# Causal block attention and a gated convolution on one core: q and k loaded nine tokens a row, the last 64 tokens with the rest, and a new written-out order

## The chip, the cores and the metric

The kernel runs on 1 core of one Trainium2 chip. The metric is the device time of one execution in microseconds (us), the median of several runs. The core has five engines that work side by side: PE (TensorE), DVE (VectorE), ACT (ScalarE), POOL (GpSimd) and SP (SyncE, which here only issues DMAs). Sixteen DMA engines move data between HBM, the on-chip SBUF and back. Matrix products land in PSUM, which has eight banks of 2 KB a partition.

## The reference

There are 8 batches, 8 heads, 576 tokens and 64 values a head, in float32. Attention is causal by blocks of 64 tokens:

```python
scores = scale * np.matmul(q, k.transpose(0, 1, 3, 2))     # scale 1/8
mask = block_i >= block_j                                  # blocks of 64 tokens
attn = softmax(np.where(mask, scores, -1e9))
x = (attn @ v)          # then [B, S, H * D] = [8, 576, 512]
gate_pre += conv_w[k] * xp[:, k:k + S, :]                  # causal, five taps, per channel
out = (1 / (1 + np.exp(-gate_pre)) * (x @ w_val)) @ w_out
```

## The kernel before, in words

Each step is one small function (an op), and the text PLAN lists all of them: `S/5.1/P/4+5` is op S with arguments 5 and 1 on engine P (PE) with PSUM banks 4 and 5. Engines: P is PE, V DVE, A ACT, G POOL, S SP. Each engine works through its own words in the order of the list and waits for what they need; so the order of PLAN is the order on every engine and on SP's queue, but engines run ahead of each other freely.

The attention works by pairs of heads, `p` = 0 to 31, four to a batch. For one pair the steps are these.

- `lq`, `lk` (L258) load the first 512 tokens of two heads into `qks` (five buffers), four tokens a row: rows of 1024 B. `lt` (L281) loads the last 64 tokens of all eight heads of a batch, two tokens a row (512 B), in two transfers each for q and k. `lv`, `lvt` (L274, L288) load v.
- `cq` casts q and k of a pair to fp16 (`qk16`), mostly on POOL; `ct` does so for the tails, `cv` and `cvt` for v. All copies and casts go through one helper, so they have the line of that helper: L244 on ACT, L246 on DVE and POOL.
- `T` turns q and k of a pair by 16 transposes on PE (L141) into half of two PSUM banks, and `Te` evacuates 1024 elements a partition into `qkT` (four buffers) on DVE or ACT, putting the tokens back in order. `TT`, `TTe` do so once a batch for the tails, into `ktails` (`kt`). The first pair has its own steps `cq0`, `T0`, `T0e`.
- `S` (three parts, t = 0, 1, 2) makes the scores transposed, keys on partitions. Both heads of a pair use a half of PE's rows. Part 2 holds keys 256 to 383 and the 64 tail queries against all four key blocks. `SL` makes the scores of the tail keys for a batch.
- `E` (L458, ACT) exponentiates 1024 elements a partition into `pt`; `EL` (L474) does so for SL. `mka` and `mkb` (L481, L483, L487, POOL) then set to zero what the mask hides.
- `A` multiplies with v, 20 matmuls; a column of ones in v gives the sums. `N` (L508, L509, DVE) divides. `X` transposes back and `Xe` writes to `xt`, channels on partitions. `AT`, `NT`, `XT`, `XTe` do the same for the tail queries of a batch.

The second half works on runs of 464 columns of `xt`, `n` = 0 to 9: `C` is the convolution by 80 matmuls of 32 rows and 32 columns with diagonal weights, `CS` (L617, ACT) its tanh, `V` the product with `w_val` (four parts of four matmuls), `Ve` (L635, DVE) the gate. `O` multiplies 128 tokens with `w_out`, `Oe` evacuates, `Od` (L660, SP) stores. `C/n` needs the columns of its run, so the first convolution waits for the first batch's attention.

PSUM is shared out by hand: a pair of banks has four quarters, and `place` puts a step into free quarters (`PAIRS`: two of them, `SINGLES`: one, the three of `A`).

Of the kernel before, what the change touches and what calls it, by code (L numbers as in the profile page):

```python
# [12 lines left out]
lk/1/S ppool//G pdve//V lcv//S ccv//G CW//P/1 lq/1/A cq/1/V T/1/P/4+5 lq/0/S lk/0/S lt/0.1/S  # L13
lt/0.0/S ct/0/G lk/4/S lq/3/S CWe//V lk/3/S cq/3/G cq0/0/V T0/0/P/0+1 lq/2/S lk/2/S lq/4/S cq0/1/V
T0/1/P/2+3 Te/1/A pact//A S/1.1/P/4+5 lv/1.0/S lv/0.0/S lv/0.1/S S/1.0/P/6+7 lt/1.0/S lq/5/S
lv/2.1/S T0e/0/V lk/5/S T0e/1/A S/0.0/P/2+3 lv/1.1/S lv/2.0/S lvt/0/S lv/3.1/S lt/1.1/S TT/0/P/0+1
lk/6/S TTe/0/V lv/3.0/S lq/6/S cq/4/G E/1.1/A E/0.0/A lwv/1/S lwv/0/S SL/0/P/0+1 EL/0/A S/0.2/P/2+3
E/1.0/A S/1.2/P/4+5 E/1.2/A S/0.1/P/0+1 T/3/P/6+7 cq/2/V T/2/P/4+5 mka/1/G cv/0/G Te/3/A S/3.1/P/6+7
E/0.1/A T/4/P/0+1 Te/2/V S/2.2/P/4+5 lwo/1/S lwo/0/S E/0.2/A mka/0/G mkb/0/G lk/7/S S/2.1/P/2+3
lq/7/S lt/2.0/S Te/4/V S/4.0/P/0+1 E/3.1/A E/2.2/A E/2.1/A S/2.0/P/6+7 E/2.0/A A/0/P/4+5 S/3.2/P/6+7  # L20
cq/5/V T/5/P/2+3 lt/2.1/S lk/8/S lv/4.1/S lq/10/S E/4.0/A N/0/V cv/2/V X/0/P/4+5 mkb/1/G cv/1/G
A/1/P/0+1 lq/8/S Xe/0/V E/3.2/A S/4.1/P/4+5 N/1/V S/3.0/P/6+7 mkb/3/G mkb/2/G mka/2/G Te/5/A
S/5.0/P/2+3 lk/10/S E/4.1/A ct/1/G cv/3/G lv/4.0/S A/2/P/0+1 N/2/V lq/9/S lk/9/S lv/6.0/S E/3.0/A
mka/3/G S/5.1/P/4+5 E/5.1/A TT/1/P/6+7 TTe/1/V lv/5.1/S cvt/0/G cq/6/G A/3/P/0+1 N/3/V cwv/1/G
cwo/0/G E/5.0/A ct/2/G lv/7.1/S S/4.2/P/6+7 SL/1/P/4+5 lv/6.1/S EL/1/A mka/4/G cq/7/G E/4.2/A
mkb/4/G cq/8/G lq/13/S lv/5.0/S lv/7.0/S lvt/1/S lk/12/S lq/12/S lk/11/S lq/11/S AT/0/P/2 X/1/P/4+5
X/3/P/0+1 Xe/3/A T/6/P/6+7 Te/6/A X/2/P/0+1 Xe/2/A NT/0/V XT/0/P/3 S/6.0/P/6+7 E/6.0/A Xe/1/V
C/0/P/0+1+4+5 CS/0.1/A CS/0.0/A XTe/0/V cwv/0/V V/0.3/P/7 cwo/1/V Ve/0.3/V V/0.0/P/6 Ve/0.0/V
S/6.1/P/4+5 E/6.1/A W//P/0+1+2+3 We/0/A We/1/V S/5.2/P/6+7 TT/2/P/4+5 TTe/2/V V/0.2/P/2 SL/2/P/0+1
S/6.2/P/4+5 E/5.2/A T/7/P/6+7 Ve/0.2/V Te/7/V EL/2/A E/6.2/A V/0.1/P/0 S/7.0/P/4+5 E/7.0/A mka/5/G  # L30
T/8/P/6+7 S/7.1/P/2+3 E/7.1/A Ve/0.1/V cv/4/G A/4/P/0+1 Te/8/V S/8.2/P/6+7 N/4/V E/8.2/A O/0.2/P/4
Oe/0.2/A mkb/5/G S/8.1/P/0+1 E/8.1/A X/4/P/2+3 mka/6/G cq/10/G Xe/4/V cq/9/G T/9/P/6+7 T/10/P/6+7
Te/9/V S/8.0/P/4+5 E/8.0/A O/0.0/P/2 Oe/0.0/V S/7.2/P/0+1 E/7.2/A S/9.2/P/4+5 E/9.2/A cv/6/G mkb/8/G
Te/10/V mkb/6/G A/6/P/2+3 cv/5/G A/5/P/0+1 N/6/V mka/7/G S/9.0/P/6+7 S/9.1/P/4+5 E/9.0/A mkb/7/G
cv/7/G A/7/P/2+3 lk/13/S E/9.1/A lt/3.0/S N/5/V X/5/P/2+3 S/10.1/P/6+7 E/10.1/A lq/14/S lt/3.1/S
cvt/1/G AT/1/P/0 S/10.0/P/4+5 E/10.0/A O/0.1/P/1 Oe/0.1/A lk/14/S N/7/V Xe/5/V NT/1/V XT/1/P/0
X/6/P/6+7 Xe/6/A XTe/1/V X/7/P/2+3 cq/12/G T/12/P/4+5 cq/11/G T/11/P/4+5 lv/9.1/S S/10.2/P/0+1
E/10.2/A cq/13/G mka/9/G Xe/7/V C/1/P/2+3+6+7 lv/8.1/S CS/1.0/A ct/3/G cq/14/G mka/8/G Te/11/V
Te/12/V lv/8.0/S lq/15/S cv/8/G mkb/9/G V/1.0/P/1 Ve/1.0/V V/1.1/P/0 Ve/1.1/V CS/1.1/A lk/15/S
lv/9.0/S lt/4.1/S S/11.1/P/2+3 lvt/2/S lv/11.1/S lt/4.0/S E/11.1/A lv/11.0/S lk/17/S T/13/P/4+5  # L40
TT/3/P/4+5 lq/17/S lv/10.0/S lv/10.1/S lq/18/S lk/18/S Te/13/V S/11.0/P/6+7 E/11.0/A V/1.3/P/1
Ve/1.3/V T/14/P/2+3 Te/14/V mkb/10/G cv/9/G lv/12.0/S mka/11/G S/11.2/P/6+7 V/1.2/P/0 TTe/3/A
E/11.2/A S/13.1/P/4+5 mkb/11/G lv/12.1/S Ve/1.2/V S/14.1/P/2+3 S/13.2/P/6+7 cq/15/G A/8/P/0+1
E/13.1/A O/0.4/P/4 ct/4/G E/13.2/A S/13.0/P/6+7 N/8/V E/14.1/A lq/16/S lk/16/S Oe/0.4/V A/9/P/0+1
S/12.0/P/2+3 X/8/P/4+5 E/13.0/A T/15/P/4+5 N/9/V S/12.1/P/6+7 S/12.2/P/0+1 E/12.0/A E/12.1/A
lv/13.1/S Te/15/V Xe/8/V X/9/P/2+3 E/12.2/A cv/11/G A/11/P/2+3 N/11/V O/0.5/P/7 lt/6.1/S Oe/0.5/A
Xe/9/V S/14.0/P/5+6 mka/10/G cvt/2/G lv/13.0/S cq/17/G TT/4/P/0+1 T/17/P/0+1 X/11/P/0+1 Te/17/V
# [12 lines left out]
V/2.2/P/2 Ve/2.0/V Xe/15/V S/19.2/P/0+1 E/19.0/A Ve/2.2/V E/19.2/A Od/0.3/S lv/17.1/S lq/24/S  # L60
cq/20/G T/20/P/6+7 mka/16/G lv/16.0/S lvt/4/S lv/19.0/S ct/5/G mkb/17/G lv/17.0/S Od/0.4/S
TT/5/P/6+7 lv/19.1/S C/3/P/2+3+4+5 CS/3.0/A Te/20/V V/3.1/P/0 V/3.0/P/1 CS/3.1/A SL/4/P/2+3 TTe/5/V
SL/5/P/2+3 EL/4/A lk/23/S cq/22/G cq/21/G lk/24/S lk/25/S EL/5/A lv/20.1/S C/4/P/4+5+6+7 CS/4.0/A
Ve/3.0/V Ve/3.1/V V/3.2/P/1 Ve/3.2/V V/3.3/P/2 S/20.2/P/4+5 lq/25/S lq/27/S CS/4.1/A lk/26/S
Od/0.2/S T/21/P/0+1 TT/6/P/0+1 lt/7.0/S Od/0.1/S cv/18/G mka/19/G mkb/16/G T/22/P/6+7 E/20.2/A
cv/16/G O/1.0/P/3 Te/22/A lk/27/S lv/21.0/S mkb/19/G S/20.1/P/4+5 E/20.1/A Ve/3.3/V O/1.1/P/2
lq/26/S lv/21.1/S mkb/18/G Te/21/V S/21.1/P/6+7 A/16/P/4+5 Oe/1.0/V TTe/6/V Oe/1.1/V S/21.0/P/2+3
N/16/V cv/17/G E/21.1/A cv/19/G A/19/P/0+1 N/19/V S/21.2/P/6+7 E/21.0/A E/21.2/A S/20.0/P/4+5
A/18/P/2+3 V/4.0/P/1 cvt/4/G cq/24/G cq/23/G N/18/V E/20.0/A mka/21/G cq/25/G Ve/4.0/V S/22.0/P/6+7
E/22.0/A X/19/P/2+3 T/24/P/2+3 Xe/19/V Te/24/V lv/20.0/S Od/0.6/S lv/22.0/S lv/22.1/S T/23/P/4+5  # L70
cq/27/G lv/23.0/S A/17/P/0+1 N/17/V lvt/6/S cv/21/G mkb/21/G V/4.1/P/6 Ve/4.1/V lt/7.1/S lk/29/S
# [12 lines left out]
O/1.5/P/6 EL/7/A A/23/P/4+5 N/23/V S/24.1/P/0+1 E/24.1/A Xe/20/V V/5.2/P/7 mkb/27/G Ve/5.2/V
# [28 lines left out]
def kernel(  # L113
# [123 lines left out]
    def rot(tiles, i):  # L237
        return tiles[i % len(tiles)]
# [503 lines left out]
```

## Time and profile before

| | us |
|---|---|
| runs, median of 3 (lowest to highest) | 183.24 (182.59 to 184.49) |
| span of the profiled execution, first to last instruction | 180.0 |
| PE busy (share of the span) | 159.7 (89%) |
| ACT busy | 137.3 (76%) |
| DVE busy | 122.6 (68%) |
| POOL busy | 82.6 (46%) |
| DMA queue of SP, share of 16 engines | 76.0% |
| granted TensorE clock | 1.000 |

How to read it: the profile shows one execution. It gives that execution's span; a time of its own beside the span is not given, and the median of the runs lies 3.24 us above it. PE busy counts a matmul from its issue to its modelled end, so a busy PE can still be waiting between matmuls. Groups of instructions are named by line, engine and out<-in. "PEld" is the loading of weights into PE, which lies beside the matmuls.

### The profile page before, as it was taken

To read this page: it belongs to the slowest core of one execution; us is meant where nothing else is said; L and a number is where in the kernel's file an instruction comes from. 1 tells how busy PE (TensorE), PEld (TensorE's weight loads), DVE (VectorE), ACT (ScalarE), POOL (GpSimd) and SP (SyncE) were. 2 spreads that over 40 slices of the span, in tenths; PEclk is the share of its full clock that TensorE was granted. 3 is DMA by queue.
4 is the path that set the end of the run, shared out by engine and by line. 5 is a ranking of instruction groups with operands and counts; after the bars stand their busy time and mean duration, and the time that the engine had idled before them with its cause. 6 is when DMAs were issued, how large, how long until landed. Compare 5 with 4: busy or idle time off the path is not lost.

```text
span 180.0 us, 8228 instructions
## 1 busy us (share of the span) xinstructions
PE 159.7 (89%) x3513; PEld 98.5 (55%) x3513; DVE 122.6 (68%) x249; ACT 137.3 (76%) x162; POOL 82.6 (46%) x198
## 2 busy tenths in 40 slices
PE   0567987779989998899899999999999999999991
PEld 0343765345754665656555755566775557455450
DVE  6635665687869786669748896587984876935640
ACT  2499999889979997989798989988996753333432
POOL 6326372677674677547467437462930622000000
PEclk9999999999999999999999999999999999999999
DMA  5899899997978799969999997998796006063366
GB/s 171 255 302 228 195 326 358 267 271 171 292 223 233 175 281 243 236 200 269 296 214 273 329 275 193 293 284 224 229 319 167 0 4 230 6 232 127 117 235 232
DMA packets 66494, 40.39 MB, mean 224 GB/s; under 512 B 40213, under 2 KB 60949, under 8 KB 66458
## 3 DMA queue, kind: packets, MB, share of 16 engines
q1 hardware_dynamic: 65898, 39.35, 76.0%
q8 instruction: 27, 0.44, 1.1%
q10 hardware_dynamic: 560, 0.52, 0.9%
q14 instruction: 9, 0.07, 0.1%
HBM read 30.42 MB, written 9.44 MB: 221 GB/s over the span
## 4 chain that ended last, share of the span: by engine, by line
PE 59%; DMA 14%; SPq 9%; ACT 6%; issue 4%; DVE 3%; POOL 2%; POOLq 0%; DVEq 0%
PE PS L137 54%; PE PS L141 5%; DMA qks<-in_q_dram 5%; ACT pt L458 4%; SPq L258 4%; DMA qks<-in_k_dram 3%; DMA vs<-in_v_dram 3%; SPq L281 3%; SPq L274 2%; DMA conv_nat<-in_moe_conv_w_dram 2%; DMA vts<-in_v_dram 2%; ACT qkT L244 1%; DVE x L509 1%; DVE qkT L246 1%; POOL qk L246 1%
## 5 line engine op out<-in xcount | busy, mean ns | idle before, releaser
L458 ACT ACTIVATE pt<-PS 128x1024 f16<-128x1024 f32 x96 | 93.1, 1041 | 10.6 <-PE PS L137 9.0
L246 POOL CAST qk<-qks 128x1024 f16<-128x1024 f32 x28 | 29.0, 1041 | 18.8 <-DMA qks<-in_k_dram 9.1
L137 PE MATMUL PS<-xt,w_val 128*128 128x464 f16 x160 | 36.5, 360 | 0.5 <-DVE w_out L600 0.3
L137 PE MATMUL PS<-qkT 64*128 64x256 f16 (+3 forms) x256 | 34.0, 319 | 3.0 <-DVE qkT L246 1.2
L137 PE MATMUL PS<-w_out,gv 128*128 128x512 f16 (+1 forms) x148 | 35.6, 374 | 0.0
L635 DVE SCALAR_TENSOR_TENSOR gv<-th,PS 128x112 f16<-128x112 f32 (+4 forms) x64 | 26.1, 449 | 10.2 <-ACT th L617 5.1
L137 PEld LDWEIGHTS <-pt 128*128 128x128 f16 (+1 forms) x960 | 28.0, 103 | 8.0 <-issue 4.0
L137 PE MATMUL PS<-v,pt 128*128 128x65 f16 (+1 forms) x896 | 31.4, 196 | 0.8 <-POOL v L246 0.3
L246 DVE COPY qkT<-PS 128x1024 f16<-128x1024 f16 (+1 forms) x24 | 28.7, 1199 | 4.7 <-PE PS L141 3.0
L137 PEld LDWEIGHTS <-qkT 64*128 64x128 f16 x512 | 17.5, 98 | 16.6 <-issue 9.4
L617 ACT ACTIVATE th<-PS 128x928 f32<-128x928 f32 x20 | 17.8, 947 | 9.9 <-PE PS L137 9.5
L246 POOL CAST v<-vs 128x512 f16<-128x512 f32 x31 | 19.2, 622 | 12.0 <-DMA vs<-in_v_dram 8.7
L509 DVE TENSOR_TENSOR x<-PS,rc 128x512 f16<-128x512 f32 x32 | 22.1, 692 | 1.1
L137 PEld LDWEIGHTS <-w_val 128*128 128x128 f16 x160 | 13.9, 98 | 14.1 <-issue 2.6
L137 PEld LDWEIGHTS <-gv 128*128 128x128 f16 x148 | 13.0, 98 | 13.3 <-issue 1.5
L246 DVE COPY osb<-PS 128x512 f32<-128x512 f32 x18 | 12.4, 690 | 7.6 <-PE PS L137 5.2
L141 PE MATMUL PS<-ident,qk 64*128 64x64 f16 x512 | 13.8, 199 | 3.9 <-POOL qk L246 1.3
L246 DVE COPY xt<-PS 128x512 f16<-128x512 f16 (+1 forms) x34 | 13.1, 399 | 5.4 <-PE PS L141 3.2
L481 POOL MEMSET pt<- 64x256 f16 x32 | 9.8, 306 | 14.0 <-ACT pt L458 13.0
L244 ACT COPY osb<-PS 128x512 f32<-128x512 f32 x17 | 10.0, 586 | 7.0 <-PE PS L137 4.5
L141 PEld LDWEIGHTS <-qk 64*128 64x128 f16 x512 | 11.1, 100 | 7.2 <-POOL qk L246 2.8
L508 DVE RECIPROCAL rc<-PS 128x8 f32<-128x8 f32 x32 | 6.6, 205 | 12.2 <-PE PS L137 9.6
(62 smaller groups left out, 134.3 us busy)
## 6 DMA issues: line engine op xcount, KB each, us to landing
out_dram<-osb SPq DMA_DIRECT2D x35, 256.0 KB, 3.3
qks<-in_k_dram SPq DMA_DIRECT2D x32, 256.0 KB, 4.7
vs<-in_v_dram SPq DMA_DIRECT2D x64, 128.0 KB, 4.3
qks<-in_q_dram SPq DMA_DIRECT2D x31, 256.0 KB, 4.6
tls<-in_k_dram SPq DMA_DIRECT2D x16, 64.0 KB, 4.1
tls<-in_q_dram SPq DMA_DIRECT2D x16, 64.0 KB, 3.6
vts<-in_v_dram SPq DMA_DIRECT2D x8, 128.0 KB, 4.0
gv<-in_moe_w_val_dram SPq DMA_DIRECT2D x2, 512.0 KB, 6.9
```

The source lines that it names most:

```text
L137: made.append(nc.tensor.matmul(out=out, lhsT=lhsT, rhs=rhs, start=start, stop=stop, skip_group_check=True))
L141: made.append(nc.tensor.transpose(out=out, in_=in_, identity=identity))
L244: i = nc.scalar.copy(out=out, in_=in_)
L246: i = (nc.vector if eng == "V" else nc.gpsimd).tensor_copy(out=out, in_=in_)
L258: DMA[eng].dma_start(out=rot(qks, p)[0:128, i], in_=(q, k)[i][b, 2 * g:2 * g + 2, 0:512, 0:64].rearrange("h (p n) d -> p h (n d)", n=4))
L281: DMA[eng].dma_start(out=tls[b % 2][0:128, i, r], in_=(q, k)[i][b, 0:8, 512:576, 0:64].rearrange("(g r) (p n) d -> r p g (n d)", r=2, n=2)[r])
L458: made.append(nc.scalar.activation(out=rot(pts, p)[0:128, 0:2, 512 * t:512 * t + 512], in_=both(take("S", p, t)), func=AF.Exp, bias=0.0, s ...
L481: nc.gpsimd.memset(pt[64:128, 0:2, 0:1024].rearrange("p h (t s) -> p h t s", t=2)[:, :, :, 0:64], 0.0)
L508: made.append(nc.vector.reciprocal(out=rc[0:128], in_=r[:, :, :, 64:65]))
L509: made.append(nc.vector.tensor_tensor(out=rot(x16, p)[0:128].rearrange("p i h d -> p h i d"), in0=r[:, :, :, 0:64], in1=rc[0:128].to_broad ...
L617: made.append(nc.scalar.activation(out=rot(ths, n)[0:128, 2 * i:2 * i + 2], in_=both(take("C", n, i))[:, :, 0:RUN], func=AF.Tanh, bias=0.0 ...
L635: made.append(nc.vector.scalar_tensor_tensor(out=gv[0:128, x, a - 4 * i:e - 4 * i], in0=rot(ths, n)[0:128, x, a - o:e - o], scalar=1.0, in ...
```

## The change

q and k are handled by units of two pairs, `u` = 0 to 15, two to a batch, with all 576 tokens. One transfer loads nine tokens a row (2304 B) of one head of each of the two pairs; the rows of the two alternate over the 128 partitions. A cast `cd` takes q or k of a unit (1152 elements a partition, `cds` half of it), `Tt` turns it by 18 transposes into three quarters of two banks, `Te` evacuates 1152 elements, `Tex` the half for one pair. The tail's own path (`lt`, `ct`, `TT`, `TTe`, `byhead`, `tls`, `tl16`, `ktails`) is gone, as are `T0`, `T0e`, `cq0` and `w0`, a matmul on zeros. The last 64 queries are read straight from `qkT`, so S's third part has 8 matmuls in place of 10, on as many columns; the places of the parts in `pt` and the two memsets follow from that. The casts and evacuations have lines L247 (ACT) and L249 (DVE, POOL) after the change.

```diff
-    qks = consts(5, [128, 2, 2, 256], fp32, "qks")
-    tls = consts(2, [128, 2, 2, 128], fp32, "tls")
-    qk16 = consts(4, [128, 4, 4, 64], fp16, "qk16")
-    qkT = consts(4, [128, 2, 512], fp16, "qkT")
+    qks = [consts(3, [128, 2, 576], fp32, f"{n}s") for n in "qk"]
+    qk16 = [consts(2, [128, 9, 2, 64], fp16, f"{n}16") for n in "qk"]
+    qkT = consts(3, [128, 2, 2, 640], fp16, "qkT")
...
-    def load_qk(i, p, eng):
-        b, g = divmod(p, 4)
+    def load_qk(i, u, h, eng):
+        b, w = divmod(u, 2)
         DMA[eng].dma_start(
-            out=rot(qks, p)[0:128, i],
-            in_=(q, k)[i][b, 2 * g:2 * g + 2, 0:512, 0:64].rearrange(
-                "h (p n) d -> p h (n d)", n=4))
+            out=rot(qks[i], u)[0:128, h],
+            in_=(q, k)[i][b, 4 * w + h:4 * w + h + 3:2, 0:576, 0:64].rearrange(
+                "x (p n) d -> p x (n d)", n=9))
...
+    def cd(u, i, eng, bank=None):
+        copy(eng, rot(qk16[i], u)[0:128].rearrange("p n h d -> p h n d"),
+             rot(qks[i], u)[0:128].rearrange("p h (n d) -> p h n d", n=9))
...
+    def Tt(u, i, eng, bank):
+        o = place(bank, TRIPLES, "Tt", u, i)
+        for n in range(9):
+            halves(both16(bank), o + 64 * n, rot(qk16[i], u)[0:128, n])
...
+    def Te(u, i, eng, bank=None):
+        bank, o = placed("Tt", u, i)
+        copy(eng, rot(qkT, u)[0:128, i, 0:2, 0:576].rearrange("p x (r s n) -> p r x s n", r=2, n=9),
+             tokens(both16(bank)[:, :, o:o + 576]))
...
     def S(p, t, eng, bank):
...
-            work = [(0, 2, 256, 512)] + [(256 + 64 * j, j, None, None) for j in range(4)]
+        work = ([(0, 0, 0, 512)], [(0, 3, 384, 512), (128, 1, 128, 512)],
+                [(0, 2, 256, 576), (320, 0, 512, 576), (384, 1, 512, 576), (448, 3, 512, 576)])[t]
...
     def mka(p, eng, bank=None):
-            pt[64:128, 0:2, 0:1024].rearrange("p h (t s) -> p h t s", t=2)[:, :, :, 0:64], 0.0)
-        nc.gpsimd.memset(pt[64:128, 0:2, 896:960], 0.0)
+            rot(pts, p)[64:128, 0:2, 0:1024].rearrange("p h (t s) -> p h t s", t=2)[:, :, :, 0:64], 0.0)
...
     def mkb(p, eng, bank=None):
-        nc.gpsimd.memset(rot(pts, p)[64:128, 0:2, 1024:1088], 0.0)
+        nc.gpsimd.memset(
+            rot(pts, p)[64:128, 0:2, 640:1408].rearrange(
+                "p h (t s) -> p h t s", t=2)[:, :, :, 0:64], 0.0)
```

The whole PLAN is written anew. The preparations that stood in two words (`ppool`, `pdve`) are cut into smaller ones (`pv`, `px`, `pt`, `pd1`, `pz`) and placed later. The first transfers go on two queues, ACT's and SP's:

```diff
-lk/1/S ppool//G pdve//V lcv//S ccv//G CW//P/1 lq/1/A cq/1/V T/1/P/4+5 lq/0/S lk/0/S lt/0.1/S
+pdve//V lq/0.1/A lq/0.0/S lk/0.0/A lk/0.1/S pact//A lv/2.1/S lq/1.1/A lv/3.1/S lq/1.0/A lk/1.0/S
+cds/0.0.1/A lcv//S cds/0.0.0/A lk/1.1/S Tt/0.0/P/0+1 cds/0.1.0/G Tex/0.0.0/A Tex/0.0.1/V lq/2.0/S
```

By count of words: POOL has 24 casts `cd` and 2 `cds` in place of 28 `cq` and 8 `ct`, and 20 `cv` in place of 31; DVE has 12 `cv` in place of 1 and 6 `cd`; ACT has 8 `Xe` in place of 3, 2 `cds` and 2 `Tex`. E, EL, CS, N, Ve, Oe, A, X, C, V and O are as many as before, on the same engines.

More of the change, by code (lines that the diff above doesn't have):

```diff
@@ L18 @@
[L18 to L23, printed above, removed]
@@ L192, in placed, with half @@
         return take(*key), 256 * zs[0]
+    def half(*key):
+        if key in halved:
+            return placed(*key)
+        halved.add(key)
+        taken.append(where[key])
+        return where[key], 256 * spots[key][1][0]
+    halved = set()
     ident = const([128, 128], fp32, "ident")
@@ L312, in pdve, with pd1 @@
         nc.vector.tensor_copy(out=ident16[0:128], in_=ident[0:128])
-        for i in range(2):
-            nc.vector.memset(ktails[i][0:128, 0:4, 1:2, 64:128], 0.0)
+    @op
+    def pd1(eng, bank=None):
         for i in range(4):
@@ L317, in pdve, with pz, pv, px @@
             nc.vector.tensor_copy(out=idfold[hs, 0, 0:32], in_=ident16[hs, 32 * i:32 * i + 32])
[L318 to L324 removed]
+    @op
+    def pz(eng, bank=None):
+        for t in qkT:
+            nc.vector.memset(t[0:128, 1, 0:2, 576:640], 0.0)
+    @op
+    def pv(eng, bank=None):
         for t in v16s:
             nc.gpsimd.memset(t[0:128, 0:4, 0:2, 64:65], 1.0)
+    @op
+    def px(eng, bank=None):
+        for i in range(4):
+            nc.gpsimd.memset(xt[0:128, 0:4, slot(i):slot(i) + 4], 0.0)
+        nc.gpsimd.memset(xt[0:128, 0:4, RING:RING + 4], 0.0)
+    @op
+    def pt(eng, bank=None):
         for i in range(2):
@@ L329, in ppool @@
             nc.gpsimd.memset(v16t[i][64:128, 0:8, 64:65], 0.0)
-        for i in range(4):
-            nc.gpsimd.memset(xt[0:128, 0:4, slot(i):slot(i) + 4], 0.0)
-        nc.gpsimd.memset(xt[0:128, 0:4, RING:RING + 4], 0.0)
         for t in vts:
@@ L383, in halves @@
             turn(out=r[:, h, o:o + 64], in_=x[hs], identity=ident16[hs, hs])
-    def transposes(t, i, r, o=0):
-        for c in range(4):
-            halves(r, o + 256 * i + 64 * c, t[0:128, c, 2 * i:2 * i + 2, 0:64])
-    def in_order(r, i):
-        return r[:, :, 256 * i:256 * i + 256].rearrange("p r (n s) -> p r s n", n=4)
-    @op
-    def T0(i, eng, bank):
-        where["T0", i] = bank
-        transposes(qk16[0], i, both16(bank))
-    @op
-    def T0e(i, eng, bank=None):
-        copy(eng, qkT[0][0:128, i].rearrange("p (r s n) -> p r s n", r=2, n=4),
-             in_order(both16(take("T0", i)), i))
@@ L675 @@
     nc.vector.memset(tiny[0:128], 0.0)
-    nc.vector.memset(wz[0:128], 0.0)
     make_identity(nc, ident)
```

286 lines of the change are left out of this document (117 added, 169 removed).

## The prediction

> **What bounds the kernel now.** I read the page's busy shares and slices first, then the stretches of time, the groups, the waits, the chain, and last the timeline for where ten landmarks fall.
>
> ```profile
> PE 159.7 (89%) x3513; PEld 98.5 (55%) x3513; DVE 122.6 (68%) x249; ACT 137.3 (76%) x162; POOL 82.6 (46%) x198
> ...
> PE   0567987779989998899899999999999999999991
> ...
> DMA  5899899997978799969999997998796006063366
> ...
> q1 hardware_dynamic: 65898, 39.35, 76.0%
> ```
>
> PE is nearly full from mid-span on; before that its digits show holes. The loads keep the DMA engines at seven to nine tenths until about 138 us. The stretches show who is full while PE is not (columns: length, PE, PEld, DVE, ACT and POOL busy, clock, DMA share, GB/s):
>
> ```profile
> 15.00:20.00 5.00, 3.94 (x56) 2.46 (x57) 2.72 (x5) 5.00 (x7) 2.29 (x8) 1.00 0.88 214
> 20.00:25.00 5.00, 4.36 (x99) 3.25 (x96) 3.27 (x8) 5.00 (x6) 2.36 (x8) 1.00 0.86 252
> ...
> 100.00:110.00 10.00, 10.00 (x227) 6.13 (x226) 8.94 (x17) 8.79 (x10) 4.98 (x10) 1.00 0.93 263
> ...
> 140.00:150.00 10.00, 10.00 (x211) 5.93 (x210) 6.79 (x17) 6.21 (x8) 5.00 (x15) 1.00 0.03 10
> ```
>
> Early on ACT is busy without a gap: it exponentiates. Later PE is. The groups give the durations that I use (busy us, mean ns | idle before):
>
> ```profile
> L458 ACT ACTIVATE pt<-PS 128x1024 f16<-128x1024 f32 x96 | 93.1, 1041 | 10.6 <-PE PS L137 9.0 <-POOL qk L246 0.8 <-POOL v L246 0.3
> L246 POOL CAST qk<-qks 128x1024 f16<-128x1024 f32 x28 | 29.0, 1041 | 18.8 <-DMA qks<-in_k_dram 9.1 <-DMA qks<-in_q_dram 6.2 <-issue 2.1
> L246 DVE COPY qkT<-PS 128x1024 f16<-128x1024 f16 x23 | 28.0, 1221 | 4.6 <-PE PS L141 2.8 <-ACT pt L474 1.5
> L246 DVE COPY qkT<-PS 128x512 f16<-128x512 f16 x1 | 0.7, 691 | 0.2 <-PE PS L141 0.2
> ```
>
> The casts wait for q and k to land (9.1 + 6.2 us). How long PE itself waits for the evacuations of the transposed q and k is in the view of the tile qkT, under what ended its engine's idle time:
>
> ```profile
>   DVE qkT L246: 3.6, 8
>   ACT qkT L244: 3.1, 7
> ```
>
> The chain runs over SP's issues and landings from 24 to 68 us and is pure PE from 88 us to the end:
>
> ```profile
> 46.52 0.54 SPq L281
> 47.07 0.04 issue
> 47.11 0.60 SPq L281
> ...
> 154.54 21.78 PE PS L137 x256
> ```
>
> The landmarks are the ten convolution blocks C/0 to C/9, found in the timeline by their 80 small matmuls:
>
> ```profile
> 29.72 1.27 PE L137 MATMUL PS<-xt,DG 32*32 32x464 f16 x80
> ```
>
> They start at 29.7, 52.0, 75.1, 87.5, 91.4, 112.6, 135.5, 148.0, 159.5 and 164.8 us. From the plan I count the work listed ahead of each, with the rows' durations: PE by start-to-start times of undisturbed steps (S 0.222, A 0.614, V 0.784, O 0.864, C 1.203, sixteen transposes 0.233 us), ACT by busy time over count (E 93.1/96 = 0.970). For C/4 that is 82.3 us of ACT and 58.6 us of PE, 91.4 us after the start. So up to C/4 time runs at 91.4/82.3 = 1.11 of the ACT work ordered ahead, while PE has lost a third: until there the kernel goes at ACT's pace, with the DMA engines close by (81 us of packet time done by then, 0.89 of the clock). After C/4 PE has 136.3 − 58.6 = 77.7 us left and takes 176.4 − 91.4 = 85.0, which is 7.3 over.
>
> **The change, part by part.** *Transfers.* Before: 64 of 256 descriptors of 1024 B, and 32 of 128 of 512 B for the last 64 tokens. After: 64 of 128 descriptors of 2304 B; the bytes are the same. The trace's packet records average 18.6, 29.6, 52.9 and 90.1 ns for 256, 512, 1024 and 2048 B. A packet of 2304 B is not in the trace. The slope from 1024 to 2048 B gives 90.1 + 256 × 0.0363 = 99.4 ns; at the bytes-per-ns of the 1024 B row it would be 119 ns, at the best single rate (2048 B, median 84 ns) 94.5. I take 99.5, as 2048 is the nearest size. Over 16 engines: before (16,384 × 52.9 + 4,096 × 29.6)/16 = 61.7 us, after 8,192 × 99.5/16 = 50.9 us; 10.8 us less of some 137, bounds 0.8 and 13.3 less.
> [...]
>
> *SP.* 32 tail issues go (L281, median 0.60 us): 19 us of queue time, in a stretch where the chain runs over just these.
>
> *POOL.* Casts 28 × 1.041 + 8 × 0.615 = 34.1 become 24 of 1152 elements at 1.041 + 128 × 0.00082 = 1.146, and 2 halves: 28.9. Eleven v casts go to DVE (−6.8 us); per pair one memset of 0.199 goes and mkb's grows to 0.306 (−2.9 us in all). POOL is at 46%; this only brings casts forward.
>
> *DVE and ACT.* An evacuation of 1152 elements costs 1.221 + 128 × (1.221 − 0.691)/512 = 1.354 us on DVE and 1.14 on ACT, in place of 1.221 and 0.72 (a tail). 32 × 1152 is the old 32 × 1024 + 8 × 512 to the element, so only fixed costs go. With the moved casts and copies DVE goes from 126.0 to 131.6 us by my count, ACT from 141.7 to 144.6 (two casts, two half evacuations, five more Xe). Neither is hidden by itself; what counts is where it stands.
>
> *PE.* 32 × 18 transposes are 31 × 16 + 2 × 8 + 8 × 8 = 576 as before. S's third part has 320 + 3 × 64 = 512 columns in 8 matmuls where it had 256 + 4 × 64 in 10; steps of equal columns took equal times (0.22 to 0.24 us for 2, 4 and 10 matmuls), so I take 0, with up to 64 × 13 ns = 0.8 us gained if instructions counted. PE's work stays at 136.1 us against 136.3.
>
> *The start.* The first four transfers now go on ACT's and SP's queues, both q heads first. The first q transfer landed 3.7 us after its issue at 0.74; with 0.58 MB for both I take 4.5. In the changed kernel's instruction list ACT's fourth load waits on the completion count that its first one raises, and the casts are queued behind it: issue 0.5 us, two casts 0.64 each, to 6.3. 18 transposes (16 cold ones took 0.61) to 6.95; the halves of the evacuation go one after the other, ACT then DVE, as DVE's waits for ACT's (0.64 + 0.76), with idfold's copies queued behind; the k transposes need the same two banks and follow at 8.4; the first E starts at about 10.1 us, 8.7 before. But six E then run back to back, where before an EL, a Te and gaps lay between: by 17 us both have about seven.
>
> *The new order.* This is the largest term. Counted as above, what stands ahead of C/4 is 73.8 us of ACT, not 82.3, and 55.2 us of PE, not 58.6: fewer exponentials run ahead of the PE work that the convolutions open. The last load that a cast listed ahead of C/4 needs stands after 64.2 us of DMA time, against 75.6.
>
> *The sum.* C/4 at 73.8 × 1.11 = 82.0, plus 1.0 for the later start: 83.0 us. The loads allow it: when C/4 started before, 81.2 us of packet time were done, 5.6 more than needed; with that lead (64.2 + 5.6)/0.89 = 78.4. PE then has 136.1 − 55.2 = 80.9 us left, with the same loss (7.3 × 80.9/77.7 = 7.6): 171.5. What follows the last matmul stays (180.0 − 176.4 = 3.6): a span of 175.1, or 4.9 less. The profiled execution is known by its span of 180.0 alone; the median of the runs, 183.24, lies 3.2 above it, and I keep that: 178.3 us.
>
> **The rivals.** *More gain.* If the freed queues also remove half of the 7.6 us that PE loses late, it is 174.5. For it: POOL's casts wait 15.3 us for q and k. Against: late in the span PE's idle time is already small.
>
> *The long rows do not move faster* (119 ns a packet, or the rows are cut into smaller packets, so that the transfer doesn't do what it says). 44 transfers are needed ahead of C/4, each 128 × 19.5/16 = 0.156 us dearer: 6.9 us. With the same lead (71.1 + 5.6)/0.89 = 86.2, and C/4 comes 3.2 later: 181.5 us. [...]
>
> *The coarse unit: slower.* Two pairs now become ready together, after four transfers, two casts and two evacuations of 1.354 us, and none of their six S can start before both. Each transposition holds three quarters of two banks where T held half. PE waits 3.6 + 3.1 us for qkT now. If each of the 13 units after the first three exposed half of its two evacuations, 1.354 us, PE would wait 17.6, or 10.9 more, and the gain turns into 183.24 − 4.9 + 10.9 = 189.2 us. It wins from (4.9 + 6.7)/13 = 0.89 us a unit. For it: DVE is the fuller engine after the change and works in order. Against: qkT holds six pairs, not four, so a unit can be prepared a unit ahead.
>
> **How the numbers follow.** Forecast 0.50, more gain 0.12, no faster rows 0.12, coarse unit 0.26. The range, 173.5 to 188.0, takes in the second and third and most of the way to the coarse unit; the forecast's own is 175 to 181.4. Faster by over 1% 0.62, within 1% (about what a measurement of this kernel can tell from none) 0.12, slower 0.26.
>
> **What would show it.** Right: 8,192 packets of 2304 B near 99 ns; C/4 near 83 us; POOL's wait for q and k below 15.3 us; first E near 10. Wrong: PE's waits for qkT above 11 us, C/4 later than 88, or idle PE after 100 us above what it is now.

## The result, and the profile after

The changed kernel takes 191.73 us (median of 4 runs, 189.31 to 193.34), the kernel before beside it 183.5: a ratio of 1.037, 95% interval 1.027 to 1.046. Forecast were 178.3 us. The profiled execution has a span of 187.5 us at a granted clock of 0.997, against 180.0. Medians below are over all runs of a kernel; the ratios compare undisturbed runs alone (of the changed kernel 189.31 and 191.25 us), with the kernel before on the same chip.

The page's busy shares, slices and queues:

```profile
PE 160.9 (86%) x3448; PEld 98.7 (53%) x3448; DVE 128.6 (69%) x254; ACT 140.6 (75%) x164; POOL 72.7 (39%) x143
...
PE   0276898998899999898699969998998899989992
...
DMA  4999998999996798599970499779975419101076
...
q1 hardware_dynamic: 53082, 38.69, 72.4%
...
q8 instruction: 27, 0.44, 1.0%
```

PE's digits are no better than before up to the middle, and where the kernel before had nines from 90 us on there is now a 6 at 89 us and another at 108 (slices 20 and 24 of 4.7 us). The stretches (columns as before):

```profile
15.00:20.00 5.00, 3.69 (x64) 2.36 (x60) 4.25 (x5) 4.11 (x6) 3.45 (x12) 1.00 1.14 319
20.00:25.00 5.00, 4.65 (x81) 3.52 (x75) 3.85 (x7) 4.08 (x5) 3.42 (x11) 1.00 1.08 316
...
90.00:100.00 10.00, 8.34 (x132) 4.00 (x115) 5.04 (x10) 7.35 (x9) 3.34 (x5) 1.00 0.75 186
...
110.00:120.00 10.00, 8.16 (x135) 4.25 (x119) 3.90 (x9) 6.44 (x7) 2.32 (x4) 1.00 0.92 275
140.00:150.00 10.00, 9.02 (x230) 6.30 (x223) 7.86 (x16) 9.12 (x11) 4.24 (x10) 1.00 0.56 173
```

ACT, which had 5.00 of 5 us in the two early stretches, now has 4.1: it no longer sets the pace there. PE, which had 10.00 of 10 in every such stretch from 90 us on, loses 1.7 and 1.8 us in two of them. The groups of the exponentials, the casts and the evacuations:

```profile
L414 ACT ACTIVATE pt<-PS 128x1024 f16<-128x1024 f32 x96 | 93.2, 1026 | 11.1 <-PE PS L136 9.9 <-DVE rc L466 0.5
...
L249 DVE COPY qkT<-PS 128x1152 f16<-128x1152 f16 (+1 forms) x24 | 31.3, 1304 | 12.1 <-ACT qkT L247 7.4 <-PE PS L140 4.6
...
L249 POOL CAST k<-ks 128x1152 f16<-128x1152 f32 (+1 forms) x15 | 17.2, 1148 | 9.2 <-DMA ks<-in_k_dram 9.0
```

The chain of waits has two pieces, in the stretches above, in which PE waits for nothing that the profile shows, and is PE alone from 170 us on:

```profile
90.35 1.66 issue
...
110.39 1.84 issue
...
170.53 13.37 PE PS L136 x68
```

C/0 to C/9 start at 31.1, 48.9, 68.7, 89.2 (C/3), 88.2 (C/4), 109.3, 134.2, 152.6, 168.1 and 169.2 us. At 88 us both kernels have done the same PE work; the changed kernel lost its time after that.

To see where, I took PE's time apart: each step's start-to-start time, less its undisturbed time (lowest tenth of like steps: S 0.22 us, A 0.60, V 0.783, O 0.863, C 0.99) and less what a change between steps of 64, 128 and 32 rows costs (0.10 us; 0.21 behind C). What is left is waiting. It is a packet end if it falls where PE's next packet of instructions is due (below) and the profile names nothing that PE waited for there; otherwise it is a wait for another engine. The column of e15 is of an execution of 186.94 us, 1.4 above its median. In us:

| | before | changed | e9, 160 in front | e10, 256 in front | e15, other order |
|---|---|---|---|---|---|
| undisturbed work of PE | 133.1 | 132.5 | | | 132.5 |
| changes of rows | 14.1 | 14.0 | 14.0 | 14.0 | 16.0 |
| up to 20 us: start and all waits | 14.3 | 15.7 | | | |
| waits, 20 to 80 us | 11.2 | 10.6 | 10.6 | 11.1 | 7.7 |
| packet ends after 20 us | 0.7 | 4.3 | 0.0 | 4.8 | 3.0 |
| waits after 80 us | 2.0 | 6.1 | 7.5 | 7.0 | 6.3 |

So the 7.5 us are 3.6 of packet ends, 4.1 of waits after 80 us less 0.6 between 20 and 80, and 1.4 in the first 20 us; PE has 0.6 less to do, and a last step that is 0.5 shorter.

### The profile page after: what moved, and what is told of

Same layout as the page of the kernel before. It is cut to its first block, busy times and chain, and to the rows that moved or that the text cites. A ratio compares the mean times of both kernels' runs of the same rounds, so it can differ in the third digit from the quotient of the medians.

```text
span 187.5 us, 8012 instructions
## 1 busy us (share of the span) xinstructions
PE 160.9 (86%) x3448; PEld 98.7 (53%) x3448; DVE 128.6 (69%) x254; ACT 140.6 (75%) x164; POOL 72.7 (39%) x143
## 4 chain that ended last, share of the span: by engine, by line
PE 66%; ACT 13%; DVE 11%; issue 4%; DMA 3%; POOL 1%; ACTq 0%; DVEq 0%; POOLq 0%
PE PS L136 60%; ACT pt L414 7%; PE PS L140 6%; DVE qkT L249 4%; ACT qkT L247 4%; DVE x L467 2%; DMA qs<-in_q_dram 2%; DVE xt L249 2%; DMA vs<-in_v_dram 1%; ACT xt L247 1%; DVE rc L466 1%; DVE gv L593 1%; ACT q L247 1%; DVE w_out L558 1%; DVE v L249 0%
## 5 line engine op out<-in xcount | busy, mean ns | idle before, releaser
L414 ACT ACTIVATE pt<-PS 128x1024 f16<-128x1024 f32 x96 | 93.2, 1026 | 11.1 <-PE PS L136 9.9
L136 PE MATMUL PS<-qkT 64*128 64x64 f16 (+4 forms) x512 | 38.5, 264 | 3.6 <-DVE qkT L249 1.0
L249 DVE COPY qkT<-PS 128x1152 f16<-128x1152 f16 (+1 forms) x24 | 31.3, 1304 | 12.1 <-ACT qkT L247 7.4
L593 DVE SCALAR_TENSOR_TENSOR gv<-th,PS 128x112 f16<-128x112 f32 (+5 forms) x64 | 26.2, 448 | 16.3 <-ACT th L575 11.0
L136 PEld LDWEIGHTS <-qkT 64*128 64x128 f16 x512 | 18.7, 99 | 21.0 <-issue 14.5
L442 POOL MEMSET pt<- 64x256 f16 x32 | 10.8, 343 | 44.3 <-ACT pt L414 44.1
L575 ACT ACTIVATE th<-PS 128x928 f32<-128x928 f32 x20 | 17.8, 946 | 8.7 <-PE PS L136 8.6
L437 POOL MEMSET pt<- 64x256 f16 x32 | 10.7, 336 | 29.8 <-ACT pt L414 29.4
L249 POOL CAST k<-ks 128x1152 f16<-128x1152 f32 (+1 forms) x15 | 17.2, 1148 | 9.2 <-DMA ks<-in_k_dram 9.0
L136 PE MATMUL PS<-xt,DG 32*32 32x464 f16 x800 | 13.5, 358 | 4.7 <-issue 3.5
L247 ACT COPY osb<-PS 128x512 f32<-128x512 f32 x17 | 10.0, 594 | 8.6 <-PE PS L136 8.6
L249 DVE COPY xt<-PS 128x512 f16<-128x512 f16 (+1 forms) x32 | 11.8, 385 | 4.6 <-ACT qkT L247 2.1
L249 POOL CAST q<-qs 128x1152 f16<-128x1152 f32 x11 | 13.2, 1202 | 4.1 <-issue 3.8
L249 POOL CAST v<-vs 128x512 f16<-128x512 f32 x20 | 13.7, 687 | 2.8 <-DMA vs<-in_v_dram 1.9
```

The costliest lines, as they stand in the source:

```text
L136: made.append(nc.tensor.matmul(out=out, lhsT=lhsT, rhs=rhs, start=start, stop=stop, skip_group_check=True))
L247: i = nc.scalar.copy(out=out, in_=in_)
L249: i = (nc.vector if eng == "V" else nc.gpsimd).tensor_copy(out=out, in_=in_)
L414: made.append(nc.scalar.activation(out=rot(pts, p)[0:128, 0:2, 512 * t:512 * t + 512], in_=both(take("S", p, t)), func=AF.Exp, bias=0.0, s ...
L437: nc.gpsimd.memset(rot(pts, p)[64:128, 0:2, 0:1024].rearrange("p h (t s) -> p h t s", t=2)[:, :, :, 0:64], 0.0)
L442: nc.gpsimd.memset(rot(pts, p)[64:128, 0:2, 640:1408].rearrange("p h (t s) -> p h t s", t=2)[:, :, :, 0:64], 0.0)
```

## The experiments

Theory at first: the new order is at fault, because it keeps fewer exponentials ahead of PE. Rivals: the wide unit of two pairs; the loads; and, from the two pieces of "issue", the instruction packets.

**Old path in the new order (e1).** The list of the changed kernel with the steps of the kernel before:

```diff
-lq/0.1/A lq/0.0/S lk/0.0/A lk/0.1/S ... cd/1.0/V ... Tt/1.0/P/2+3 ... Te/1.0/V
+lk/1/A lq/1/S lk/0/A lq/0/S lt/0.1/S lt/0.0/S ... cq/2/V ... T/2/P/2+3 ... Te/2/V
```

> The new order with the old data path: per-pair loads of 1024 B rows, casts, sixteen transposes and evacuations of 1024 elements stand where the changed kernel has its loads, casts, transposes and evacuations (two pairs for each unit, on the same engines and banks), the tails by their old path, S's third part and the memsets as before; qkT and qks have six buffers. Theory 'wide unit' (evacuations of a unit wait for each other and hold three quarters of two banks, and the first unit is late): it comes back to 182 to 185 us or better, C/0 before 29 us. Theory 'order' (the new order itself starves PE between 90 and 170 us): it stays at 189 to 193 us, with PE's late idle time as in the changed kernel. Theory 'loads' (rows of 2304 B are slow and SP stands behind stores): packets of 1024 B bring back at most 2 us, 187 to 190.

Measured: 194.21 us, ratio 1.060 (1.052 to 1.069). The new order is slow without the wide unit too; but the old path stands in it as a guest, so this proves less than it seems, as the next run shows. Its trace also has four gaps of PE at packet ends (below), 5.3 us in all.

**New path in the old order (e5).** The reverse, with four units in `qkT`:

```diff
-    qkT = consts(3, [128, 2, 2, 640], fp16, "qkT")
+    qkT = consts(4, [128, 2, 2, 640], fp16, "qkT")
```

> The order of the kernel before, carrying the new data path: units of two pairs, 2304 B rows, 16 units of casts, transpositions and evacuations, no tail path, the start of the changed kernel with its two load queues, qkT with four units. The words of exponentials, A, X, C, V, O, stores and v stand as in the kernel before. If the order is what lost the time (theory: PE stands in its list behind exponentials that are only just done, since fewer run ahead), idle PE after 100 us falls back toward that of the kernel before, and the run comes out at 180 to 184.5 us, at or under the kernel before. If the wide unit itself loses it (rival: two pairs become ready at once, banks held by three quarters), it stays at 188 us or more, whatever the order. Between 185 and 187.5 both would have a share.

Measured: 232.19 us, ratio 1.27. The theory misses by 48 us; by the words of the expectation this is the rival's outcome. The row of S on the page of this run shows where a good part of it goes:

```profile
L136 PE MATMUL PS<-qkT 64*128 64x64 f16 (+4 forms) x512 | 42.5, 279 | 25.5 <-DVE qkT L249 15.1
```

PE waits 15.1 us for evacuations on DVE, where the changed kernel has 2.1 for both engines: in an order written for pairs a unit's casts, turns and evacuations come just ahead of its first S, one behind the other. In this order the wide unit does cost PE time. What it costs in an order that prepares each unit well ahead, this run cannot tell.

**C/3 away from C/4, AT/4 away from C/5 (e2).**

```diff
-C/4/P/0+1+2+3 ... C/3/P/4+5+6+7 ... CS/4.0/A ... S/19.2/P/6+7 S/18.0/P/0+1
+C/4/P/0+1+2+3 ... S/19.2/P/6+7 S/18.0/P/4+5 ... CS/4.0/A ... V/4.3/P/2 ... C/3/P/4+5+6+7
```

> The changed kernel with C/3 moved away from C/4 (S, V/4.0, V/4.2 and V/4.3 stand between) and AT/4 moved behind C/5 and A/20. Theory 'instruction fetch' (two idle stretches of 1.7 and 1.8 us in C/3 and C/5 are PE running out of instructions in a dense run of small matmuls): both stretches go, and 2 to 3.5 us of time with them: 186 to 189.5 us. Theory 'order otherwise': the idle time reappears at other places, 190 to 193 us.

Measured: 189.39 us, ratio 1.032 (1.024 to 1.039). Both gaps are gone, but waits for other engines rose from 25.7 to 29.5 us over the whole list: moving the steps gave nearly all of it back, and the span is 187.3 us, against 187.5.

**The loads left out (e3, e4).** Both kernels without the transfers of q and k after the first:

```diff
+        if u > 2:
+            return
```

> The changed kernel without the q and k loads after the first three units (later units are computed from what lies in the buffers): some 50 us of DMA time less. Theory 'loads': it gains 5 us or more, to 186 us or below. Theories 'wide unit' and 'order': it stays within 2 us of the changed kernel.

> The kernel before without the q and k loads after the first five pairs and without the tail loads after the first two batches: some 50 us of DMA time less. If loads set the pace between 30 and 90 us there, it gains 3 to 8 us (175 to 180 us); if not, it stays within 1.5 us of 183.5. The difference between this and the changed kernel without its loads is what path and order cost with loads left out: 7 us if loads are not the cause, below 3 us if they are.

Measured: 187.40 and 179.89 us. Both kernels gain 3 to 4 us without the loads, so these do cost time. But the distance stays 7.5 us with the loads gone from both, so the rows of 2304 B, whatever they cost, do not make the difference.

**Another start (e6).**

```diff
-pact//A lv/2.1/S lq/1.1/A lv/3.1/S lq/1.0/A lk/1.0/S cds/0.0.1/A lcv//S cds/0.0.0/A
+pact//A lq/1.1/S lq/1.0/S lk/1.0/S cds/0.0.1/A lcv//S cds/0.0.0/V
```

> The changed kernel with another start alone: the third and fourth load on ACT go to SP's queue, so that ACT's casts are not queued behind a load that waits for an earlier one; one of the first two casts goes to DVE; the k transposes take banks of their own; two v loads stand later. First exponential at about 9.5 us in place of 11.0. If the late start is carried to the end (PE starts 1.0 us later than before and never gets it back), the run is 1.0 to 1.5 us shorter: 190.2. If the early part is bound by something else, by loads above all, it is within 0.5 us of the changed kernel.

Measured: 190.99 us, ratio 1.043, within 0.8 us of the changed kernel; the first S came 0.9 us later, not earlier, as the k halves were cast on POOL after a later landing. Inconclusive on what the start is worth.

**Orders with exponentials further ahead (e7, e8).** For instance, e8 lists C/0 later, with more E ahead of it; it starts at 44.9 us there, and at 31.1 in the changed kernel:

```diff
-... C/0/P/4+5+6+7 ...
+... C/0/P/0+1+4+5 ...
```

> The changed kernel with its first 28 words as they are and all the others in another order: the same steps on the same engines with the same buffers, only the places in the list (and the PSUM banks) differ. S and E stand earlier against A, C, V and O, so that more exponentials are done ahead of the PE work that needs them: C/0 stands some 12 us later, 26, 54 and 65 E have begun at 40, 80 and 100 us where the changed kernel has 21, 48 and 58. If the order is the cause (PE waits in its list behind exponentials that are only just done), the time falls: laid out with the rows' durations, the list ends 4.8 us earlier, so 184 to 186 us. If the wide unit is the cause, or DVE's and ACT's extra casts and copies, which all stay, nothing of that is gained: 188.5 to 191.

> As in the run before, the wide units and the first 28 words stay and the others are ordered anew, but copies and casts may also change engine: all six casts of q and k from DVE to POOL, seven of v too, five Oe and two Xe from ACT to DVE, two Te from ACT to DVE. ACT has some 5.5 us less and DVE some 5.5 us less to do, POOL 14 more. If the order and the share of the engines are all that was lost, the list ends by the rows' durations 10.5 us earlier than the changed kernel: 178 to 181 us, under the kernel before. If the wide unit costs PE time in any order (its three quarters of two banks, its two evacuations in a row), the run stays at or above the kernel before, 183.5 or more.

Measured: 199.70 and 197.39 us, ratios 1.093 and 1.073: far off, in the other sense. By 80 us 53 and 51 exponentials had begun (48 in the changed kernel), so these orders did run further ahead. The account by steps names two things that I had left out. The orders have 178 and 167 changes of rows where both kernels have 129: 18.8 and 17.8 us where they pay 14. And packet ends cost 2.5 and 6.1 us, among them one of 3.0 us at AT/1 in e8. A backlog of exponentials alone is not what is missing.

**Instruction packets (e9, e10).** PE has 3,448 matmuls, each with its weight load: 6,896 instructions, for which the page shows 27 packets of 0.44 MB in all, 16 KB each. I take 256 instructions for a packet, an estimate from these two counts: 27 × 256 is 16 more than PE has. Counted from the first, the gap inside C/3 begins 185 instructions behind 13 × 256, that inside C/5 183 behind 16 × 256. The timeline of PE in the changed kernel:

```profile
88.20 2.15 PE L136 MATMUL PS<-xt,DG 32*32 32x464 f16 x136
92.01 0.58 PE L136 MATMUL PS<-xt,DG 32*32 32x464 f16 x24 [1.66 <-issue]
...
109.34 1.05 PE L136 MATMUL PS<-xt,DG 32*32 32x464 f16 x61
112.23 0.57 PE L136 MATMUL PS<-xt,DG 32*32 32x464 f16 x19 [1.84 <-issue]
```

C/4 and C/3 run 160 matmuls, 320 instructions, in a row; the last 24 stand behind the gap. The packets began to arrive at 89.49 and 109.88 us, 2.5 and 2.4 us ahead of PE's going on. The edit puts small matmuls, read by nobody, into the time in which PE waits for the first load (80 in e9, 128 in e10):

```diff
+    @op
+    def w0(n, eng, bank):
+        for _ in range(n):
+            mm(one(bank)[:, 0:64], ident16[0:64, 0:128], ident16[0:64, 0:64])
...
-pdve//V lq/0.1/A
+pdve//V w0/80/P/7 lq/0.1/A
```

> The changed kernel with 80 small matmuls, whose result nobody reads, as the first thing on PE, in the 5 us in which PE waits for the first load; all else stays. The trace of the changed kernel shows 27 packets of instructions of 16 KB for 6,896 instructions of PE, so 256 a packet, and its two long gaps without a cause on PE both begin 183 to 185 instructions behind a multiple of 256, inside C/3 and C/5. Theory: PE stands there because it has used up one packet before the next has come, and 160 more instructions ahead shift these places to stretches with fewer instructions a microsecond: the two gaps of 1.7 and 1.8 us go, none takes their place before C/9, and the run is 1.5 to 4 us shorter than with 256 more, unless PE then waits that much longer for other engines. Rival: the gaps come from C itself or from what the convolution waits for; then they stay at C/3 and C/5.

> The same with 128 small matmuls, 256 instructions: a whole packet more, so that the places fall where they fell. The gaps inside C/3 and C/5 are there again, within 0.6 us of their size, and the time is that of the changed kernel, 189.5 to 192. If the small matmuls gain or lose something in themselves (PE is busy earlier), both shifted kernels differ from the changed kernel in the same sense, and the difference between the two still tells what the gaps cost.

Measured: 186.90 us (ratio 1.030, 1.021 to 1.040) and 191.74 us (1.056, 1.042 to 1.070). The timelines, first of e9, then of e10:

```profile
87.98 2.61 PE L136 MATMUL PS<-xt,DG 32*32 32x464 f16 x160
...
107.49 1.27 PE L136 MATMUL PS<-xt,DG 32*32 32x464 f16 x80
```

```profile
94.27 0.58 PE L136 MATMUL PS<-xt,DG 32*32 32x464 f16 x24 [1.70 <-issue]
...
114.26 0.57 PE L136 MATMUL PS<-xt,DG 32*32 32x464 f16 x19 [1.60 <-issue]
```

With 160 instructions in front both convolution stretches run through, and e9 has no gap of this kind of over 0.3 us after 20 us; with 256 the gaps are back before the same 24 and 19 matmuls, in an unchanged order with unchanged data. So the gaps hang on the place in PE's stream of instructions. What they cost can't be read from e9 against e10, though, for the small matmuls of e10 run longer than PE's idle time (start of PE's timeline, first e9, then e10):

```profile
1.63 4.44 PE L136 MATMUL PS<-ident 64*128 64x64 f16 x80 [1.63 <-DVE ident L307]
6.27 0.66 PE L140 MATMUL PS<-ident,q 64*128 64x64 f16 x18 [0.20 <-ACT q L247]
```

```profile
1.62 6.90 PE L136 MATMUL PS<-ident 64*128 64x64 f16 x126 [1.62 <-DVE ident L307]
...
8.40 0.71 PE L140 MATMUL PS<-ident,q 64*128 64x64 f16 x16
```

The first transposes begin 2 us later in e10, and C/4 starts at 90.4 us in e10, 88.0 in e9 and 88.2 in the changed kernel. Of the 5.2 us between the spans of e10 and e9 (189.5 and 184.3), 2.4 were there before the first of the two gaps. The changed kernel is the better partner: level with e9 at C/4, it ends 3.2 us later (187.5). That is what the two gaps cost in these traces; by the table they are 4.3 us, of which 1.4 came back as waits after 80 us. The ratios alone, measured on different chips, would not show it: 1.030 (1.021 to 1.040) for e9 and 1.037 (1.027 to 1.046) for the changed kernel.

**A second pair of orders (e11, e12)**, written with the row changes and packet ends counted:

```diff
-... C/0/P/4+5+6+7 ...
+... C/0/P/6+7+0+1 ...
```

C/0 starts at 42.6 us in e11 and 53.4 in e12; the lists have 124 and 117 changes of rows.

> A second order for the changed kernel, same first 28 words, same steps on the same engines. As in the first such run the exponentials run further ahead (C/0 some 9 us later; 26, 54, 66 E begun at 40, 80, 100 us, where the changed kernel has 21, 48, 58), but two things that the traces of those runs showed are taken into account: PE loses 0.10 us at each change between steps with 64 rows (S, X, transposes) and with 128 (A, V, O), so changes are kept at 124, not 178 (the changed kernel has 129), and no stretch of some 300 instructions of PE is shorter than 6 us. If the order is the cause, it ends 4 to 6 us earlier than the changed kernel, 184 to 187.5. If the wide unit is, or DVE's and ACT's extra casts and copies, 188.5 or more.

> As in the run before, but casts and copies may change engine too (as in the earlier pair: q and k casts all on POOL, most v casts too, some Oe, Xe and Te from ACT to DVE); 117 changes of step kind, and exponentials further ahead (28, 58, 67 E begun at 40, 80, 100 us). If order, engine shares, changes of kind and instruction packets are the whole loss, it ends 7 to 10 us earlier than the changed kernel: 180 to 184, level with or under the kernel before. If the wide unit costs PE time in any order, 185 or more.

Measured: 197.62 and 190.53 us, ratios 1.088 and 1.049. Missed again: row changes fell to 13.7 and 12.9 us and packet ends to 1.2 and 1.4, but PE's other waits were about 36 and 31 us (25.7 in the changed kernel). These orders let several steps share a pair of banks, and an evacuation was seen to wait for a step written into its pair ahead of it in the list: after X/9 in e8, N/10 on DVE stood 2.0 us until that X had run, and X/10 on PE 1.1 us for N/10. How much of the 36 and 31 us comes from this was not counted.

**What is left: banks, DVE's casts, order (e13 to e16).** Behind 80 small matmuls, nothing but 62 PSUM banks changed in e13, nothing but the engine of 19 casts in e16; e14 and e15 have new orders with the same engines, e15 without small matmuls:

```diff
-X/12/P/4+5 ... X/14/P/6+7 ... A/19/P/0+1 ... X/31/P/6+7
+X/12/P/2+3 ... X/14/P/4+5 ... A/19/P/2+3 ... X/31/P/2+3
...
-cd/1.0/V ... cv/0/V ... cv/6/V cv/7/V ... cvt/5/V
+cd/1.0/G ... cv/0/G ... cv/6/G cv/7/G ... cvt/5/G
```

> The kernel with 80 small matmuls in front (186.9 us), every word at its place, but 62 of its PE steps in other PSUM banks, so that an X no longer stands in the pair of a Tt or A whose evacuation is still to come, and an A or S follows no late evacuation. If what is left of the loss is PE waiting for banks (A/14 0.9 us for Xe/12, A/16 0.8 for Xe/14, A/26 0.7, X/31 0.6), the run is 2.5 to 4.5 us shorter: 182.5 to 184.5, level with the kernel before. If DVE's casts or the order are the cause, PE waits at the same places for the same engines whatever the bank: 186 or more.

> With the same 80 small matmuls, same steps on the same engines and the first 28 words kept; banks and places both changed, each move kept only where the list, laid out with the rows' durations, the packets of 256 instructions and the banks' evacuations, ends earlier. Laid out so it ends 10 us before the kernel with 80 small matmuls. Earlier orders came out 4 to 6 us later than laid out. If order and banks are all of the loss and neither the wide unit nor DVE's extra casts cost anything that an order can't hide, 178 to 182 us, under the kernel before. If they do, 184 or more.

> The same kind of order without small matmuls in front: the places are chosen so that no packet of instructions ends in a dense stretch. Laid out it ends 2 us later than the run before. If packets, banks and order are the cause, 180 to 184; if the small matmuls help in another way (PE busy earlier), it is more than 4 us above the run before.

> The kernel with 80 small matmuls in front, order and banks as they are, but the 19 casts that stand on DVE (12 of v, 6 of q and k, one of the v tails) on POOL, most of which the change moved to DVE. If DVE's load is what makes N, Xe and Te late, PE's waits after 80 us fall by half and the run is 2 to 4 us shorter, 183 to 185. If the banks or the order are, it is within 1 us of 186.9, or longer where a cast now stands behind other casts on POOL.

Measured: e13 186.69 us (ratio 1.011, 1.004 to 1.018), e14 186.92 (1.008, 1.001 to 1.014), e15 185.54 (1.009, 1.003 to 1.014), e16 189.56 (1.027, 1.020 to 1.033). The times of e13 and e14 lie in the ranges of their rivals and that of e15 just above its theory's, but by the ratios, each with the kernel before on the same chip, all three are level with it within 2%. Moving the casts gains nothing: DVE is 12.5 us less busy (116.1 us), PE's waits after 80 us are about 7 us as before, and the ratio is e9's within its interval. DVE's casts are not why PE waits there. For the banks, PE's waits from 78 us on, in e9 and then in e13:

```profile
PE PS L136 <- ACT xt L247: 0.8, 1, 0.8
...
PE PS L136 <- DVE xt L249: 0.7, 1, 0.7
```

```profile
PE PS L136 <- DVE v L249: 0.4, 1, 0.4
PE PS L136 <- ACT qkT L247: 0.3, 1, 0.3
```

The waits for Xe are gone, but others stand in their place: 7.5 us after 80 us as in e9, and the spans are 184.3 and 184.4. The ratio, on another chip than that of e9, says a gain of 2%. I call it unclear.

The main result is e15. It has the changed kernel's steps, engines and buffers, and no small matmuls; nothing but the order and the banks differ. It stands at 1.009 (1.003 to 1.014), where the changed kernel stands at 1.037 (1.027 to 1.046). So most of the loss belongs to the list, and not to the wide unit or to the shares of the engines. With e13 and e14 it shows that the new path can come to within some 1% of the kernel before; none went under it.

**A last order (e17)**, some copies and casts on other engines:

```diff
-Oe/0.2/A ... cd/2.1/V ... cv/12/V
+Oe/0.2/V ... cd/2.1/G ... cv/12/G
```

> The changed kernel's steps, buffers and first 28 words, in an order in which no 300 instructions of PE take less than 6.5 us where a packet ends, with some copies and casts on other engines (six Oe casts and copies from ACT to DVE, four casts of v, two of q or k and a tail from DVE to POOL). Laid out with the rows' durations it ends 1 us earlier than the order of e15. If the order was the cause and the new path has a gain to give, 179 to 182.3 us, under the kernel before. If the new path gives no gain and costs nothing in a fitting order, within 1% of the kernel before, 182.3 to 185.5. If the wide unit costs time in any order, above 185.5.

Measured: 186.67 us, ratio 1.022 (1.017 to 1.028): by the words of the expectation, the wide unit's range. But the list loses 2.7 us at a packet end inside C/5 in the profiled run, which it was written to avoid, so this is no test of the unit. No order with the new path was faster than the kernel before.

## Why the prediction was wrong

The step that failed is the largest term, the new order: "up to C/4 time runs at 1.11 of the ACT work ordered ahead", hence C/4 at 83.0 us, and from there "the same loss", 7.6 us. C/4 came at 88.2, so 1.20 of the 73.8 us; and PE then needed 95.7 us for its 80.9, a loss of 14.8. These two are 5.2 + 7.2 = 12.4 us, which is what the end of PE is off (183.9 for 171.5).

- The 1.11 was measured on an ACT that was busy nearly without a gap, 37.1 of the 40 us from 10 to 50 us. In the new order it was busy 33.7 of them and waited for PE's scores, and by 90 us 54 exponentials were begun instead of 60. A ratio measured while an engine is full can't be carried to an order that doesn't fill it. That the smaller lead is itself the cause is not shown: e7 and e8 had a larger one and were slower.
- The loss after C/4 was taken over from a list whose steps and packets happen to fit. It belongs to the list, not to the work: 3.2 us of it go with 160 instructions in front (e9), and in another order of the same steps the kernel comes from 1.037 to 1.009 (e15).
- *Transfers.* 8,192 packets of 2304 B took 117.6 ns in the mean (99.5 forecast), the value of the second rival; the packet time of all is 141.6 us, before 140.8. The median is 93 ns. In the kernel before the rate rose with the size, 17.3, 19.4 and 22.7 B per ns in the mean at 512, 1024 and 2048 B; 2304 B moved at 19.6 in the mean, beside 22.6 of the 2048 B packets in the same trace. By the medians it is 24.8 against 24.4. Why 2304 B moved more slowly in the mean than 2048 B is not shown. The term was worth nothing, but e3 and e4 show that it isn't why the kernel is slower.
- *SP.* The queue is gone from the chain, as said. Evacuations on ACT and DVE took its place there, and at 88 us both kernels stood level.
- *POOL, DVE, ACT, PE.* Right: casts of q and k 30.4 us (28.9 forecast), POOL's wait for them 9.0 (15.3 before); Te 1.354 us on DVE and 1.119 on ACT (1.354 and 1.14); DVE's busy time up 6.0 and ACT's 3.3 (5.6 and 2.9); PE's work 0.6 less (0 to 0.8).
- *The start.* First E at 10.98 us (10.1 forecast), and by 20 us 8 exponentials done against 10, where I had both level by 17 us.
- *The rivals.* The coarse unit's 189.2 us is close to the result by luck, by another road: it asked for waits of PE for qkT above 11 us, and the groups that waited on the tile qkT show 7.1 us for PE and its weight loads together:

```profile
  PEld L136: 2.8, 4
  PE PS L140: 2.2, 2
  PE PS L136: 2.1, 4
```

  Its cost appeared where the order doesn't fit it (e5). The other two signs of failure, C/4 later than 88 us and more idle PE after 100, came true.

What is settled: most of the loss is the list's, not the data path's (e15), and two packet ends are part of it, 4.3 us by the account and 3.2 us of the span against e9. Not settled is how the rest, PE's short waits after 80 us above all, divides between order and banks; loads and DVE's casts are not it. In the best of these orders (e14 and e15) a loss of 0.1 to 1.4% is left, whose cause stays open; the wide unit may be it.

## What to carry to other kernels

When an order changes, cost the new order by itself: neither an engine's pace nor the bound engine's waiting carries over from the old list (here 1.11 became 1.20, and a loss of 7.6 us 14.8). Count instructions, not only microseconds: where a trace shows gaps that nothing explains, look whether they fall at a fixed place behind multiples of the packet (some 256 instructions here), and shift the stream by some idle instructions before anything else is blamed. See that these fit into the idle time: the 80 small matmuls did, the 128 did not. And a test that puts one half of a change into the frame of the other half measures the misfit, so fit the frame or don't conclude.

## What the runs showed of the hardware

- PE's 6,896 instructions came in 27 packets of 16 KB in the changed kernel, some 256 in each, and PE stood still where the next packet came late. In the nineteen traces there are 34 gaps of PE of over 0.35 us after 20 us for which the profile names nothing that PE waited for. All stand 183 to 191 instructions behind a multiple n × 256, and PE went on 2.2 to 3.1 us after the transfer of the n-th packet began. They were 1.7 and 1.8 us in the changed kernel, up to 2.8 in e8; a packet itself took 0.9 to 1.8 us in the changed kernel, among the loads. That PE waited for the packet there is read from these places and from the two shifted runs: with 160 instructions in front (e9) both gaps were gone, with 256 (e10) they were back, 1.7 and 1.6 us. In the changed kernel the n-th packet began to arrive between 3.1 us before and 1.7 us after PE's passing instruction n × 256.
- S, of 64 rows, behind a step of 128 rows started 0.10 us later than another step of 128 rows did: V behind V starts after 0.783 us, S behind V after 0.879; O 0.863 and 0.959. X, of 64 rows too, started 0.873 us after O, so not every change shows the 0.10 us.
- DVE's casts from fp32 were longer in the changed kernel, where DVE has more of them (12 of v for 1) and POOL casts beside it. In the kernel before, DVE's one cast of 512 elements of v took 419 ns. The rows of the changed kernel:

```profile
L249 DVE CAST v<-vs 128x512 f16<-128x512 f32 x12 | 6.6, 555 | 0.0
...
L249 DVE CAST k<-ks 128x1152 f16<-128x1152 f32 x2 | 2.9, 1436 | 0.0
...
L249 DVE CAST v16t<-vts 128x512 f16<-128x512 f32 x1 | 1.4, 1362 | 0.0
```

  As many elements took 555 ns in the mean and once 1,362. That POOL's casts beside them are the cause was not tried by itself.
